# Letting planned transfers go by TensorE products instead of by queue order alone

## The chip, the cores and the metric

The kernel runs on one core of a Trainium2 chip. The metric is the device time of one execution in microseconds (us). A core has five engines with their own instruction streams: TensorE (PE, with its weight loads shown as PEld), VectorE (DVE), ScalarE (ACT), GpSimd (POOL) and SyncE (SP). Transfers are issued from the streams of SP, ACT and POOL, and move on 16 DMA engines.

## The reference

The kernel computes a DeltaNet attention block and then an MLP block. Cut to what matters:

```python
k_n = k / (norm(k) + 1e-06)                       # 4 batches, 8 heads, 768 steps, 48 wide
for t in range(S):
    y[t] = q[t] @ state
    v_old = k_n[t] @ state
    state = state + beta[t] * outer(k_n[t], v[t] - v_old)
x = y.transpose(0, 2, 1, 3).reshape(4, 768, 384)
xn = (x - mean(x)) / sqrt(var(x) + 1e-06) * g_ln
out = x + maximum(xn @ w_ch1, 0) @ w_ch2          # 384 -> 1536 -> 384
```

The two weight matrices arrive as 64-bit floats; the kernel makes 32-bit floats of them.

## The kernel before, in words

The 768 steps are cut into 12 chunks of 64 steps (`C = 64`). Inside a chunk the recurrence becomes matrix algebra: the products of the keys with each other (`gram`, line 963, stored to DRAM by the `gd<-gsb` transfers), the inverse of a unit triangular matrix per head, the chunk's corrected values (`recur`), the output `y` and the new state `s_all`. The chunks follow each other through `s_all`. Chunk 0 is inverted on PE (`first_inverse`, lines 915 and 930). For chunk 1 and for later pairs of chunks (`rows_inverse`) SP reads blocks of the stored products back (`gb<-gd`), ACT takes a root of their diagonal (`nrm_b`, line 1026), DVE goes through the rows one by one (lines 1045 and 1050, tiles `tmp` and `xb`), and the result goes out to DRAM (`xd<-xb`) and back in another layout (`xt<-xd`). Chunk 1 is joined from blocks of 16 (`blocks_join`, lines 1071 to 1089: `xnj` on DVE, then products on PE), the others from blocks of 32 (`join`, lines 1103 to 1125).

After `recur(c)` comes the MLP of the chunk's 256 tokens, `mlp(c)`: for chunks 0 to 2 the first product is plain (line 1483, ReLU on ACT in line 1492), later ones use a scheme of eleven products (line 1416); the second product is plain in chunk 0 (line 1505) and otherwise uses a scheme of seven products (line 1584), with sums on POOL and DVE (lines 1570, 1602, 1609).

The loads around the change are these. `load_raw` brings a chunk's keys to `kr` (for chunk 3 to `tb`), `load_padded` and `load_blocks` bring queries or keys to `tb`, `load_v` the values, `norms` reads the diagonal of the stored products (`ksum<-gd`), and eight small loads bring `beta_b`. SP issues nearly all of them. POOL issues the keys of the later chunks (`load_blocks(..., "Pool")`). ACT issues the twelve weight loads of 768 KB (`words<-in_moe_w_ch_dram` and two to `h_all`); `convert` turns each into weights with ACT, DVE and POOL (lines 730 to 748).

The order of all this is not written out by hand. Every piece of work is a `Step` of a `Line` with an engine, a cost and a priority. `schedule()` plays the engines and DMA queues through with costs in us and gives each step a planned start and end. A step may have `t0`, the time before which the plan doesn't start it:

```python
load_raw(c, pr=pr, t0=27.0)
...
load_padded(1, q, 1, ("SP", "SP"), pr=8.2, t0=42.0)
load_v(1, pr=8.1, t0=42.0)
...
t0 = {2: 85.0, 3: 105.0}.get(c, 0.7)
```

`emit()` (line 391) then issues the steps in the order of their planned starts, and `in_this_order` keeps that order on each engine. In the kernel before, `t0` has no other effect on the chip: an instruction whose operands and buffers are ready, and whose semaphore is free, runs as soon as its engine reaches it, whatever time the plan had for it. Each transfer from SP or ACT uses one of eight semaphores in turn, and a transfer waits until the one before it on the same semaphore has landed.

Of the kernel before, what the change touches and what calls it, by code (L numbers as in the profile page):

```python
# [23 lines left out]
@contextmanager  # L24
def in_this_order(tc):
    first = len(tc.nc.cur_bb.bb.instructions)
    last = {}
    yield last
    queued = None
    for ins in tc.nc.cur_bb.bb.instructions[first:]:  # L30
        if ins.engine not in ORDERED:
            continue
        if ins.engine in last:
            tc.add_manual_dep(
                ins, last[ins.engine].name,
                mybir.DependencyInfo(mybir.DependencyClass.NoSync, mybir.DependencyReason.DATA),
                reason="in_this_order",
            )
        last[ins.engine] = ins
        if "DMA" in type(ins).__name__ and ins.engine != mybir.EngineType.Pool:  # L40
            if queued is not None and queued.engine != ins.engine:
                tc.add_manual_dep(
                    ins, queued.name,
                    mybir.DependencyInfo(mybir.DependencyClass.NoSync, mybir.DependencyReason.DATA),
                    reason="in_this_order",
                )
            queued = ins
# [27 lines left out]
class Line:  # L75
# [313 lines left out]

        self.steps = every + self.fills  # L390

    def emit(self):
        for s in sorted(self.steps, key=lambda s: (s.start, s.n)):
            s.fn()


@with_exitstack
def kernel(
# [116 lines left out]
    line = Line()  # L515
# [1200 lines left out]
    for n, (p0, c, rows, cols) in enumerate(spots(BK, (0, 1))):  # L1716
        e, t0 = rows.start // C, c * C + cols.start
# [53 lines left out]
    if PLAN is not None:  # L1771
        PLAN.append(line)
    with in_this_order(tc):
        line.emit()


# [28 lines left out]
```

## Time and profile before

| | |
|---|---|
| runs | 558.52 us (median of 3; 556.83 to 559.81) |
| the profiled execution | 561.34 us |
| its span, first to last instruction | 559.0 us |
| PE busy / DVE / ACT / POOL | 525.5 / 370.3 / 192.1 / 253.2 us |
| granted TensorE clock, mean | 0.980 |
| PE share of the chain that ended last | 78% |
| DMA engines, mean rate | 98 GB/s |
| instructions | 23060 |

All times inside the execution are counted from its first instruction. In profile lines "SPq" stands for SP issuing a transfer; the time beside it is how long the issuing instruction took, not the transfer. Where a helper issues every transfer, all have its line, L555; the tile names tell them apart (`tb<-in_q_dram` is a load of queries to `tb`), without the buffers' numbers. A wait is named by what came last before the waiting instruction started.

### The profile page before, as it was taken

The page shows a single profiled execution, that of the slowest core. Times are in us where ns is not written, and L with a number is a line of the kernel's source. Part 1 is how long each engine was busy: PE and PEld are TensorE (multiplying, and loading weights), DVE is VectorE, ACT ScalarE, POOL GpSimd, SP SyncE. Part 2 cuts the span into 40 slices and gives each one's busy share as a digit, 9 for nine tenths or more (in the row PEclk, how much of TensorE's full clock was granted, in tenths as well). Part 3 has the DMA queues.
Part 4 walks back from the last instruction along what each step waited for, and adds up shares of the span by engine and source line. Part 5 has one row for each costly group of instructions (what it writes and reads, how often), then busy time and mean ns, then how long its engine had stood idle before and what let it go on. Part 6 is the DMA issues. An engine that isn't in the chain of part 4 may idle for free.

```text
span 559.0 us, 23060 instructions
## 1 busy us (share of the span) xinstructions
PE 525.5 (94%) x10060; PEld 478.8 (86%) x10060; DVE 370.3 (66%) x884; ACT 192.1 (34%) x452; POOL 253.2 (45%) x399
## 2 busy tenths in 40 slices
PE   7668869899998999899999999999999999999996
PEld 4547657678987899899999999999999999999996
DVE  5666549991689936889858968668777436253331
ACT  5667644232232324232323332513322224323030
POOL 5252337407885656267270352452352522426242
PEclk9898899999998999899999999999999999999999
DMA  9784784269454786553652543834404410111101
GB/s 177 265 158 128 195 219 64 44 149 168 55 86 71 139 195 86 106 100 83 162 77 50 99 81 77 191 46 81 94 15 103 106 30 33 32 48 40 28 1 28
DMA packets 195972, 54.65 MB, mean 98 GB/s; under 512 B 186136, under 2 KB 189344, under 8 KB 195872
## 3 DMA queue, kind: packets, MB, share of 16 engines
q1 hardware_dynamic: 190112, 40.39, 37.8%
q10 hardware_dynamic: 3552, 9.63, 5.0%
q0 software_dynamic: 2208, 3.17, 3.2%
q8 instruction: 78, 1.28, 1.0%
q14 instruction: 22, 0.18, 0.1%
HBM read 36.38 MB, written 16.78 MB: 95 GB/s over the span
## 4 chain that ended last, share of the span: by engine, by line
PE 78%; DVE 7%; DMA 6%; SPq 4%; issue 2%; ACT 1%; POOL 0%; DVEq 0%; POOLq 0%; ACTq 0%
PE f L1584 28%; PE f L1416 25%; PE f L1483 6%; SPq L555 4%; PE two L963 4%; DVE xb L1050 2%; DVE tmp L1045 2%; PE by L1222 2%; PE two L1215 2%; PE by L1160 2%; PE two L1160 2%; DMA gd<-gsb 2%; PE two L1232 2%; PE f L1505 1%; PE by L1115 1%
## 5 line engine op out<-in xcount | busy, mean ns | idle before, releaser
L1584 PE MATMUL f<-w_sb,h_all 128*128 128x192 f32 x396 | 95.0, 332 | 0.0
L1584 PE MATMUL f<-words,h_all 128*128 128x192 f32 x396 | 93.1, 328 | 0.0
L1570 POOL TENSOR_TENSOR h_all<-h_all 128x256 f32<-128x256 f32 x99 | 73.0, 742 | 43.3 <-PE f L1584 37.1
L1416 PE MATMUL f<-xnt,w_sb 128*128 128x128 f32 x648 | 88.8, 279 | 0.0
L1609 POOL TENSOR_TENSOR words<-h_all 128x128 f32<-128x128 f32 x66 | 30.3, 472 | 121.0 <-ACT h_all L1435 101.5
L1416 PEld LDWEIGHTS f<-xnt,w_sb 128*128 128x128 f32 x648 | 81.0, 193 | 0.7
L1438 DVE TENSOR_TENSOR h_all<-f,h_all 128x256 f32<-128x256 f32 x135 | 56.5, 421 | 34.1 <-PE f L1416 20.2
L1050 DVE TENSOR_TENSOR xb<-xb,tmp 128x60 f32<-128x60 f32 (+19 forms) x170 | 73.4, 432 | 5.8
L1045 DVE TENSOR_TENSOR tmp<-xb,gb 128x60 f32<-128x60 f32 (+19 forms) x170 | 65.3, 384 | 7.1 <-POOL xb L1034 4.5
L1584 PEld LDWEIGHTS f<-words,h_all 128*128 128x128 f32 x396 | 68.3, 190 | 0.4
L1584 PEld LDWEIGHTS f<-w_sb,h_all 128*128 128x128 f32 x396 | 66.4, 190 | 1.6 <-issue 0.2
L1483 PE MATMUL f<-xnt,w_sb 128*128 128x256 f32 x216 | 51.7, 390 | 0.0
L1483 PEld LDWEIGHTS f<-xnt,w_sb 128*128 128x128 f32 x216 | 41.3, 195 | 7.2
L555 POOL DMA_DIRECT2D tb<-in_k_dram x64 | 41.7, 656 | 7.0 <-DVE kt L943 5.8
L1602 DVE TENSOR_TENSOR o<-f,x 128x192 f32<-128x192 f32 x33 | 11.7, 355 | 47.7 <-PE f L1584 28.4
L1435 ACT ACTIVATE h_all<-f 128x256 f32<-128x256 f32 x54 | 20.6, 381 | 53.8 <-PE f L1416 28.0
L1584 PE MATMUL f<-w_sb,words 128*128 128x192 f32 x132 | 32.5, 330 | 0.6 <-DVE o L1602 0.6
L1602 POOL TENSOR_TENSOR o<-o,words 128x192 f32<-128x192 f32 x22 | 13.3, 624 | 38.6 <-DVE words L1602 38.6
L1492 ACT ACTIVATE h_all<-f 128x256 f32<-128x256 f32 x36 | 13.8, 383 | 38.2 <-PE f L1483 38.0
L1435 ACT ACTIVATE h_all<-h_all 128x256 f32<-128x256 f32 x54 | 22.2, 413 | 11.3 <-DVE h_all L1438 11.2
L748 POOL TENSOR_TENSOR w_sb<-words 128x768 uint32<-128x768 uint32 (+1 forms) x11 | 14.9, 1356 | 24.3 <-ACT words L738 19.4
L825 POOL TENSOR_TENSOR v<-v,knrm 128x768 f32<-128x768 f32 x11 | 16.7, 1518 | 16.7 <-DMA v<-in_v_dram 16.0
(235 smaller groups left out, 941.3 us busy)
## 6 DMA issues: line engine op xcount, KB each, us to landing
words<-in_moe_w_ch_dram ACTq DMA_DIRECT2D x10, 768.0 KB, 7.2
gd<-gsb SPq DMA_DIRECT2D x11, 512.0 KB, 3.9
v<-in_v_dram SPq DMA_DIRECT2D x24, 192.0 KB, 4.2
out_dram<-o SPq DMA_DIRECT2D x48, 96.0 KB, 2.3
kr<-in_k_dram SPq DMA_DIRECT2D x46, 96.0 KB, 3.0
xld<-xlt SPq DMA_DIRECT2D x9, 384.0 KB, 3.7
xnt<-xld SPq DMA_DIRECT2D x36, 96.0 KB, 3.0
gb<-gd SPq DMA_DIRECT2D x40, 64.0 KB, 3.7
```

Of the source, the lines that this page charges most:

```text
L555: add(eng, cost, lambda: QUEUE[eng].dma_start(out=out_, in_=in_), r, w, bulk=n * ns / 16e3, **kw)
L963: nc.tensor.matmul(pair[hp][half(e ^ (hp & n)), (g * NP + j) * C : (g * NP + j + 1) * C], kt[drows(hp), l], rt[drows(hp), i],)
L1045: nc.vector.tensor_tensor(out=t, in0=xv[:, 0:n, j : j + 1].to_broadcast([128, n, w]), in1=gv[:, j : j + 1, j + 1 : L].to_broadcast([128, n ...
L1050: nc.vector.tensor_tensor(out=rest, in0=rest, in1=t, op=ALU.subtract)
L1416: nc.tensor.matmul(wide(p[:, 128 * n : 128 * n + 128]), w[:, f : f + 128], r, start=start and n == 0, stop=stop, skip_group_check=True)
L1435: add("ACT", act(256), lambda: nc.scalar.activation(to[0], p, ACTF.Relu), pk, to[1])
L1438: add("DVE", dve(256), lambda: nc.vector.tensor_tensor(out=to[0], in0=ps(p), in1=y[0], op=op), [*pk, *y[1]], to[1])
L1483: nc.tensor.matmul(p[:, 0:TOK], w1_sb[:, t, f * 128 : (f + 1) * 128], xnt[:, t], start=(t == 0), stop=(t == KC - 1))
L1570: add(eng, cost, lambda: e.tensor_tensor(out=out_, in0=x, in1=y, op=op), r, w, port=2 if eng == "Pool" else 1, pr=-2)
L1584: lambda f=f, t=start and f == 0: nc.tensor.matmul(p[:, 0:D2], lhs(f), rhs[:, f], start=t, stop=(f == F2 - 1), skip_group_check=True),
L1602: lambda: e.tensor_tensor(out=out_, in0=a, in1=b_, op=ALU.add), r, w, pr=pr,
L1609: lambda f=f + i: e.tensor_tensor(out=s3[f], in0=one(0, 0)[0](f), in1=one(1, 0)[0](f), op=ALU.subtract),
```

## The change

`emit()` now adds waits. It walks through the steps in planned order and keeps the last instruction of each PE step with the step's planned end. For a transfer that has a set time (`t0` over 1 us), is not ACT's, and is planned to start less than 3 us after that time, it takes the latest of the last eight PE steps that end, in the plan, no later than the transfer starts, and makes the transfer wait for that step's last instruction on the chip. The plan itself, the order on each engine, and all computation stay as they are. 37 transfers get such a wait, 27 on SP and 10 on POOL. The wait is carried out by the issuing engine in its instruction stream.

```diff
-    def emit(self):
+    def emit(self, tc):
+
+        block = tc.nc.cur_bb.bb.instructions
+        gate, ends = None, []
         for s in sorted(self.steps, key=lambda s: (s.start, s.n)):
             s.fn()
+            if s.eng == "PE":
+                ends.append((s.end, block[-1]))
+            if s.bulk is not None and s.t0 > 1.0 and s.eng != "ACT" and s.start < s.t0 + 3.0:
+                gate = [i for e, i in ends[-8:] if e <= s.start]
+                if gate:
+                    tc.add_manual_dep(
+                        block[-1], gate[-1].name,
+                        mybir.DependencyInfo(mybir.DependencyClass.Sync, mybir.DependencyReason.DATA), reason="paced",
+                    )
...
-        line.emit()
+        line.emit(tc)
```

## The prediction

> **What bounds the kernel now.** I read the page's slices first, then the stretches between the places where they change, then who waits for whom in the part where TensorE is not full, and last the SP queue in order of time, because the change adds waits to it and to GpSimd's queue. The page's slices:
>
> ```profile
> span 559.0 us, 23060 instructions
> ...
> PE   7668869899998999899999999999999999999996
> ...
> DMA  9784784269454786553652543834404410111101
> ```
>
> TensorE (PE) is at six to eight tenths up to about 84 us and near full afterwards. In stretches (busy us of PE, PEld, DVE, ACT, POOL, then clock, DMA share, GB/s):
>
> ```profile
> 112.00:142.00 30.00, 30.00 (x406) 23.59 (x398) 17.14 (x41) 9.05 (x24) 12.98 (x23) 1.00 0.84 155
> 142.00:300.00 158.00, 153.78 (x3072) 142.47 (x3071) 124.39 (x279) 47.43 (x114) 91.52 (x141) 0.98 0.54 101
> ```
>
> From 112 us on PE has work all the time, so a microsecond won or lost before 112 us should reach the end one for one. Before it two stalls are the transfers' own (waits between 30 and 112 us: us in total, times, longest):
>
> ```profile
> DVE xnj L1071 <- DMA tb<-in_q_dram: 8.2, 1, 8.2
> ...
> PE f L1077 <- DVE xnj L1071: 4.4, 1, 4.4
> ACT nrm_b L1026 <- DMA gb<-gd: 4.3, 1, 4.3
> ...
> PE by L930 <- DVE nrm_b L1028: 3.7, 1, 3.7
> ```
>
> At 41.25 us ACT gets the last `gb` blocks, and PE stands for 3.7 us behind it. At 81.83 us DVE gets the `xt` blocks that `xnj` reads (the row names `tb`, which is queued right behind them), and PE stands for 4.4 us. The SP queue around both:
>
> ```profile
> 34.02 1.12 SPq L555 DMA_DIRECT2D gb<-gd  x2
> 35.23 1.84 SPq L555 DMA_DIRECT2D tb<-in_q_dram  x2
> 37.78 3.71 SPq L555 DMA_DIRECT2D v<-in_v_dram  x2
> 41.53 7.27 SPq L555 DMA_DIRECT2D beta_b<-in_beta_dram  x6
> ```
> ```profile
> 69.37 5.17 SPq L555 DMA_DIRECT2D xt<-xd  x8
> 74.64 1.16 SPq L555 DMA_DIRECT2D tb<-in_q_dram  x2
> 75.84 5.92 SPq L555 DMA_DIRECT2D v<-in_v_dram  x2
> ```
>
> Both late transfers are followed at once by loads that the plan sets for 42 and 46 us, and for 85 and 90 us: the chip issues them up to 7 and 10 us before their planned time, while its products run 4 to 10 us behind theirs.
>
> **What the change moves.** The order on every engine stays. 37 transfers (27 on SP, 10 on POOL) get a wait for a product. I matched each product with its matmuls in the trace and compared its end with the transfer's issue. 16 of the products are done before the issue: nothing moves. Four are 0.3 to 0.6 us late (one `kr` load at 28.5, one `v` half at 115.0, two k loads on POOL at 149.8 and 150.4). 17 bind, in three places:
> (a) two `tb`, two `v` and six `beta_b` loads, from 35.2-48.2 to 46.0-51.9 us (the products are L930's at 45.13+0.86, L915's at 47.2, L930's at 50.2 and 51.3, L771's at 51.9);
> (b) two `tb`, two `v` and two `ksum` loads, from 74.6-84.1 to 92.8-98.2 us, with four ungated `tb` loads among and behind them;
> (c) one `v` half, from 111.1 to 114.8 us.
>
> **Gain at gb.** In the DMA packets of the trace the last 64-byte packet of `gb` starts at 40.04, and the blocks land at 41.18: 1.14 us, while 192-byte packets of `tb` and `v` are moving. For the first six `gb` blocks the last packet is at 28.98 and the landing at 29.30: 0.32 us. I take the difference, 0.8 us. Bounds: nothing, if ACT's weight load at 33.91 is the cause alone; 3.7 us, PE's whole stall. **Gain at xt.** The last packet starts at 80.67, the landing is at 81.70: 1.03 against 0.32, so 0.7 us. ACT's weight packets in the same rings take 125 ns up to 80.2 and 145 to 260 ns from 80.25 to 81.4, when the 192-byte packets of `v` begin: a second sign that the followers cost something, and only at the end. Bounds: nothing to 4.4 us. I take the small values because the followers are the smaller part of the traffic: three weight loads of 768 KB (71.87, 72.37, 74.44) stay where they are, and `gb` has `kr` and `tb` loads ahead of it in its own queue.
>
> The Trainium skill ("DMA: Bandwidth & Descriptors", Queues, rings and completion order) says that an engine takes one ring's descriptors in order and turns between rings. That speaks against the change: a load issued later on SP's queue would not hold back an earlier one, and by it both gains are zero. The same page (Latency and other measured facts) gives HBM latency as 0.2 us on average and 2 us at high load; an estimate from that is up to 1.8 us for each landing, 3.6 us in all. No row here separates the two; the packets above lie between.
>
> **Cost of (a).** Behind the waiting loads on SP stand the store `gd` at 51.17, the store `gd` at 56.78 and the `gb` reads at 60.88. At 0.60 to 0.65 us for an issue, the four loads are out by 48.6, `beta_b` from 50.2 to 53.8, the first `gd` at 53.8 (2.6 us later), two more `beta_b` by 55.4. The second `gd` waits for ACT's copy that ends at 56.7 in any case, so SP has caught up with 1.3 us to spare. Readers: `tb` at 63.93 (L771), `v` at 74.04 (L825), `beta_b` at 82.46 (L1031), all over 10 us later. Cost 0, or 0.7 us if issues are held up as at 37.78, where one took 2.59 us. **Cost of (b).** SP has nothing else to do between 86.9 and 106.37 (`kr`). Ten issues from 92.8, the last two after `ksum` at 98.2, end near 100.7. Readers: `ksum` at 108.11 (L1144) and `tb` at 118.6 (L943); at 3.9 us to landing, 4.7 us are to spare. **Cost of (c).** The `gd` store behind it, released by ACT at 114.6, goes out about 0.9 us later, and `xd` at 124.27 waits for DVE's rows that end at 124.2. Cost 0. **POOL.** 0.3 us twice near 150 us, ahead of L1570, while PE has work: 0, at most 0.3. The 0.6 us at 28.5 shifts `kr`, `tb` and then `gb` issues, but their queue is backed up (one issue took 1.44 us at 31.18): 0, at most 0.6. **The waits themselves.** 20 more wait-only instructions (16 SP, 4 POOL) at 0.02 us in the rows of before: 0.3 us on SP, in its idle time.
>
> What takes up the delayed loads is free room, mean DMA share in the last column but one:
>
> ```profile
> 36.00:42.00 6.00, 2.37 (x70) 1.70 (x65) 2.29 (x6) 1.61 (x6) 0.31 (x2) 1.00 1.06 215
> 76.00:83.00 7.00, 2.63 (x57) 2.03 (x58) 1.17 (x3) 3.25 (x6) 0.24 (x1) 1.00 1.05 280
> 46.00:56.00 10.00, 8.85 (x336) 7.42 (x336) 7.32 (x29) 8.54 (x18) 2.59 (x3) 1.00 0.25 76
> 92.00:104.00 12.00, 10.90 (x337) 7.92 (x337) 11.41 (x25) 3.49 (x6) 9.57 (x15) 1.00 0.28 56
> ```
>
> **Sum.** -0.8 - 0.7 + 0 = -1.5 us. The profiled execution took 561.34 us (span 559.0 and 2.34 around it), so 559.8 on its own scale. The median of the runs is 558.52, 2.8 below it; I give the time on that scale: 557.0. What is late next: after 81.8 the rows of L1045 and L1050 on DVE (21.07 of 22 us busy from 90 to 112) move up with `xnj`, so the gain should not be lost there.
>
> **Rivals.** (1) The followers are the cause of both stalls. Then `gb` lands near its median of 3.0 us (issue at 34.69) and `xt` near its 2.5 us (issue at 72.68), and both PE stalls go: 3.7 + 4.4 = 8.0 us, to 550.5; with half of it 4.0 us, to 554.5. For it: DMA share over 1 in just these two windows, and 9.0 us to landing for the last `xt` block. Against it: the weight loads, which stay. It counts as faster from 2.8 us. Chance 0.37. (2) Slower: SP is not free in time in (a). The second `gd` takes 4.6 us to land (56.78 to 61.33) and its reader issues at 63.05, so from 1.7 us of lateness on every further microsecond goes through the `gb` reads, L1027, the `xd` store and `xt` to PE's stall at 78. Four of the ten issues held up as one `v` was (2.59 us in place of 0.62) put SP 7.9 us behind the 55.4 worked out above, so the second `gd` 6.5 us late, of which 4.8 reach the end: 563.3, or 561.8 if my gain is kept. Chance 0.18. (3) The waits change nothing, since the planned products end before the issue, as 16 of 37 do, or followers don't matter: 558.5. It shares 0.45 with my forecast.
>
> **How the numbers follow.** About 0.5% (2.8 us) is what a measurement of this kernel can tell from no change, so faster means under 555.7 and slower over 561.3. My forecast, with its own range 555.7 to 558.8, and rival 3 lie within: 0.45. Rival 1 gives 0.37 faster and rival 2 0.18 slower. For 8 in 10 the low end goes to 552.5 (rival 1 with 6 of its 8 us) and the high end to 560.8 (the bounds of the costs of (a), POOL and `kr`, 1.6 us together, with no gain, and part of rival 2).
>
> **What would show it.** Right: SP's `tb` and `v` at 46 and near 92 us with PE named as releaser; the wait of L1026 shorter by about 0.8 and that of L1071 by 0.7 us; the second `gd` still issued when ACT's copy ends; PE full after about 110 us. Wrong: either stall gone altogether or unchanged, `gd` or the `gb` reads issued later against ACT and DVE, L1144 or L943 waiting for a DMA, or new idle time of PE after 112 us.

## The result and the profile after

The changed kernel takes 558.96 us (median of 20 runs, 555.44 to 563.46); the kernel before, run beside it, takes 558.69 us (20 runs, 554.65 to 562.06). The ratio is 1.0009, with a 95% interval of 0.9984 to 1.0033: no difference that this measurement can tell. 557.0 us had been predicted, a ratio of 0.9973 to the median that it was worked out from. The call "no change" holds; the gain of 1.5 us behind it lies outside the interval. Runs more than 1.5% above the fastest of the same kernel count as slow and are left out of all medians and ratios below; none of these 40 is one.

The profiled execution of the changed kernel took 560.08 us, its span 557.7. Twelve lines were added ahead of the code in question, so L1071 of before is L1083 here, L1026 is L1038, L1077 is L1089, L930 is L942 and L963 is L975. First the page's slices of the kernel after:

```profile
span 557.7 us, 23080 instructions
...
PE   7669869999998999899999999999999999999996
...
DMA  9765863569455676453652544734414410111101
```

PE's row has the same shape: six to nine tenths in the first slices, then full. In the DMA row, with 14 us to a slice, the third digit (28 to 42 us) and the sixth (70 to 84) fell from 8 to 6, and the fourth, fifth and eighth (98 to 112) rose by 1, 1 and 3: the loads moved as ordered. The same stretches as before, from the kernel after (us, then PE, PEld, DVE, ACT, POOL busy, clock, DMA share, GB/s):

```profile
36.00:42.00 6.00, 2.40 (x70) 1.73 (x66) 2.32 (x6) 1.59 (x6) 0.44 (x1) 1.00 0.63 156
46.00:56.00 10.00, 8.89 (x344) 7.35 (x336) 8.98 (x29) 8.92 (x19) 3.04 (x3) 1.00 0.57 106
76.00:83.00 7.00, 2.28 (x45) 1.73 (x47) 1.25 (x3) 3.29 (x5) 0.24 (x1) 0.77 0.64 219
92.00:104.00 12.00, 10.50 (x336) 7.68 (x335) 11.41 (x25) 2.75 (x6) 9.15 (x14) 1.00 0.87 117
112.00:142.00 30.00, 29.53 (x361) 23.12 (x362) 16.71 (x40) 8.99 (x24) 12.99 (x23) 1.00 0.82 158
```

The reader is to set two columns against each other. The DMA share in the two stalls fell from 1.06 to 0.63 and from 1.05 to 0.64, and rose in the stretches that were to take the loads up. PE's busy time in the two stalls did not move: 2.40 of 6 us (2.37 before) and 2.28 of 7 us (2.63 before; the granted clock was 0.77 in this stretch, 1.00 before). The transfers went where the change sent them, and nobody waited less. The waits between 30 and 112 us, kernel after:

```profile
DVE xnj L1083 <- DMA xt<-xd: 9.7, 1, 9.7
...
ACT nrm_b L1038 <- DMA gb<-gd: 5.4, 2, 4.4
...
PE f L1089 <- DVE xnj L1083: 4.7, 1, 4.7
...
PE by L942 <- DVE nrm_b L1040: 3.6, 1, 3.6
```

The first row now names `xt` itself, since the `tb` loads that used to land with it are gone, but the wait is still there and ends at 81.75 us (81.83 before). ACT gets the last `gb` at 41.29 (41.25). PE's two stalls are 4.7 and 3.6 us (4.4 and 3.7). The SP queue, kernel after:

```profile
35.30 1.71 SPq L567 DMA_DIRECT2D gb<-gd  x2
46.15 1.32 SPq L567 DMA_DIRECT2D tb<-in_q_dram  x2
47.56 2.00 SPq L567 DMA_DIRECT2D v<-in_v_dram  x2
50.44 4.92 SPq L567 DMA_DIRECT2D beta_b<-in_beta_dram  x6
55.47 0.52 SPq L567 DMA_DIRECT2D gd<-gsb  x1
56.04 1.57 SPq L567 DMA_DIRECT2D beta_b<-in_beta_dram  x2
57.79 0.48 SPq L567 DMA_DIRECT2D gd<-gsb  x1
...
69.74 4.92 SPq L567 DMA_DIRECT2D xt<-xd  x8
93.03 0.88 SPq L567 DMA_DIRECT2D tb<-in_q_dram  x2
```

The two long gaps are SP's waits for PE products, as the waits of the SP queue between 40 and 104 us say:

```profile
SPq L567 <- PE f L1495: 18.1, 1, 18.1
SPq L567 <- PE f L1674: 9.6, 1, 9.6
```

For 9.1 us behind the `gb` reads and for 18 us behind the `xt` reads SP now issues nothing, and both still land as late as they did. So in these two profiles the loads behind them were not what made them late. What remained is what was in the queues ahead of them, above all the traffic of the other queue. DMA queues in the stretch from 73 to 80 us (packets, MB, share of 16 engines; q1 is SP's queue, q10 ACT's), kernel before and then kernel after:

```profile
q10 hardware_dynamic: 757, 2.22, 87.8%
q1 hardware_dynamic: 842, 0.06, 8.2%
```
```profile
q10 hardware_dynamic: 760, 2.24, 86.0%
q1 hardware_dynamic: 919, 0.06, 9.1%
```

ACT's weight loads take 86 to 88% of the engines' time in both, and SP's small packets get through at 1.1 to 1.2 for each weight packet of about 3 KB. In the 2 us before the weight packets begin, the trace of before shows 503 and 549 of the 64-byte packets of `xt` in a microsecond; beside them, from 75 to 79 us, 96 to 150.

### The profile page after: what moved, and what is told of

The parts are those of the page before. It is cut to its first block, busy times and chain, and to the rows that moved or that the text cites. A ratio compares the mean times of both kernels' runs of the same rounds, so it can differ in the third digit from the quotient of the medians.

```text
span 557.7 us, 23080 instructions
## 1 busy us (share of the span) xinstructions
PE 524.5 (94%) x10060; PEld 477.8 (86%) x10060; DVE 369.6 (66%) x884; ACT 191.7 (34%) x452; POOL 253.1 (45%) x399
## 4 chain that ended last, share of the span: by engine, by line
PE 80%; DVE 6%; DMA 5%; ACT 3%; issue 3%; SPq 2%; POOL 0%; ACTq 0%; DVEq 0%; POOLq 0%
PE f L1596 28%; PE f L1428 25%; PE f L1495 4%; PE two L975 4%; PE f L1517 3%; DVE xb L1062 2%; SPq L567 2%; PE by L1234 2%; PE by L1172 2%; PE two L1172 2%; PE two L1227 2%; DVE tmp L1057 2%; PE two L1244 2%; DMA xt<-xd 1%; PE by L1127 1%
## 5 line engine op out<-in xcount | busy, mean ns | idle before, releaser
L1450 DVE TENSOR_TENSOR h_all<-f,h_all 128x256 f32<-128x256 f32 x135 | 56.5, 421 | 34.1 <-PE f L1428 20.3
L1062 DVE TENSOR_TENSOR xb<-xb,tmp 128x60 f32<-128x60 f32 (+19 forms) x170 | 74.9, 441 | 5.8
```

Source lines behind the costliest of these rows:

```text
L1062: nc.vector.tensor_tensor(out=rest, in0=rest, in1=t, op=ALU.subtract)
L1450: add("DVE", dve(256), lambda: nc.vector.tensor_tensor(out=to[0], in0=ps(p), in1=y[0], op=op), [*pk, *y[1]], to[1])
```

## The experiments

My theory after the result: a small read on SP's queue that is issued behind one of ACT's 768 KB weight loads waits for that load, and what SP issues after the read does not matter. Rival: the loads that follow do matter, in one of the two places, and something in the change eats the gain. Second rival: the waits gain something and lose it again on SP. None of the kernels below leaves any computation out. Unless it says otherwise, ratios are to the kernel before on the same chip, with 95% intervals.

**The kernel before, in the changed code (one profile).** The code of the change with a condition that is never true, to see how far one profile differs from the next.

```diff
-            if s.bulk is not None and s.t0 > 1.0 and ...
+            if False and s.bulk is not None and s.t0 > 1.0 and ...
```

> The changed kernel with every new wait left out, so the program of the kernel before once more. It tells how much of the difference between the two profiles is chance: in the profile of the changed kernel the first gb read was issued 2.2 us later (25.63 against 23.46), ahead of any new wait. If that is chance, this run can have it at either place, and ACT's wait before L1038 and DVE's before L1083 end within 1 us of 41.25 and 81.83 all the same. If the followers on SP's queue held gb and xt back (rival 1), a run with the late first gb read should end ACT's wait about 2 us later than 41.3.

One run of 561.58 us, span 559.9. Last `gb` at 41.19, PE's stall behind it 3.6 us; `xnj` at 80.24, PE's stall 2.8 us. So the first stall repeats to 0.1 us, and the second varies by some 1.6 us from profile to profile: more than the 0.7 that I had predicted for it.

**Only the waits of place (a) (5 rounds).**

```diff
+            if s.t0 in (42.0, 46.0) and s.bulk is not None and s.t0 > 1.0 and ...
```

> Only the waits of the transfers planned for 42 and 46 us. My theory now: the followers cost gb nothing that can be seen and the waits push the second gd store about 1 us back, so the ratio to the kernel before is 1.000 to 1.003, with the second gd issued near 57.8 and the last xt block on its way when v and tb (still at 75 us) follow it, and DVE's wait ending at 81.5 to 82.5. Rival (followers hold gb back, and the gain was lost at SP): ACT's wait ends 0.8 us or more before 41.25 in this profile, ratio 0.998 or less.

Median 560.17 us, ratio 1.0026 (0.9989 to 1.0063). `gb` is used 6.35 us after its last issue with no follower behind it (6.56 before), PE's stall is 3.4 us, and the second `gd` goes out 1.6 us after ACT's copy that releases it. No gain in (a); a cost at the end isn't shown either, since the interval holds 1.

**Only the waits of place (b) (5 rounds).**

```diff
+            if s.t0 in (85.0, 90.0) and s.bulk is not None and s.t0 > 1.0 and ...
```

> Only the waits of the transfers planned for 85 and 90 us. With (a) left alone, SP's gd stores and gb reads are where they were, so the xt reads are issued from 69.4 as before and nothing but the followers is taken away from behind them. Rival (followers hold xt back): DVE's wait ends 0.7 us or more before 81.83, at 81.1 or earlier, and the ratio is 0.998 or less. My theory now (ACT's three weight loads hold xt back, the followers do not): DVE's wait ends at 81.4 to 82.2, PE's stall stays at 4.2 to 4.8 us, ratio 0.999 to 1.001.

Median 558.90 us, ratio 1.0003 (0.9962 to 1.0043): no gain in (b). Its profile, of a run of 556.52 us, is the surprise: PE's stall at `gb` is 0.5 us, though the followers of (a) are all there, ungated. Here are the rows of the SP queue, then of ACT's stream, then two of ACT's stream in the kernel before:

```profile
33.45 1.11 SPq L567 DMA_DIRECT2D gb<-gd  x2
34.66 1.32 SPq L567 DMA_DIRECT2D tb<-in_q_dram  x2
```
```profile
35.12 0.33 ACTq L567 DMA_DIRECT2D words<-in_moe_w_ch_dram  x1
...
36.98 1.14 ACT L885 COPY xt<-by 128x256 f32<-128x256 f32 x3
38.15 0.23 ACT L1038 ACTIVATE nrm_b<-gb 128x16 f32<-128x16 f32 x1
```
```profile
33.91 0.36 ACTq L555 DMA_DIRECT2D words<-in_moe_w_ch_dram  x1
...
41.25 0.23 ACT L1026 ACTIVATE nrm_b<-gb 128x16 f32<-128x16 f32 x1 [4.34 <-DMA gb<-gd]
```

In this run the last `gb` read went out at 34.12, a microsecond ahead of the weight load; in the kernel before it went out at 34.69, behind the weight load of 33.91. L1038 starts when ACT has finished its copies, with no wait for a DMA at all. A tenth of a microsecond behind `gb` the `tb` loads follow, and do no harm that shows: the last 64-byte packet of `gb` starts at 35.90, 1.8 us after the last issue (5.35 us in the kernel before).

**Three weight loads behind the `xt` reads (5 rounds).** The kernel before, without any wait; the weight loads of pieces 9 to 11 are issued by SP after the eight `xt` reads.

```diff
+        last = max(n for n, s in enumerate(order) if s.name == "xt1")
+        early = [s for s in order[:last] if s.name == "fetch9"]
+        order = [s for s in order[: last + 1] if s.name != "fetch9"] + early + order[last + 1 :]
...
-        add(eng, cost, lambda: QUEUE[eng].dma_start(...
+        add(eng, cost, lambda: QUEUE["SP" if kw.get("name", "") in ('fetch9', 'fetch10', 'fetch11') else eng].dma_start(...
```

> The kernel before, without any new wait, but the last three weight loads (pieces 9 to 11, 768 KB each, issued by ACT at 71.9, 72.4 and 74.4 us) are issued by SP, behind the eight xt reads; plan and order of all else as before. If ACT's weight loads hold xt back: the last xt block lands 2 to 3 us after its issue, at 75 to 76, PE's stall of 4.4 us before L1089 is gone, and the time falls by 3 to 4.4 us (ratio 0.992 to 0.995), less if DVE then waits for the later weights. If the followers on SP's queue hold it back (rival 1): they are still there, behind the weights, so the stall stays or shrinks by under 1 us, ratio 0.999 or more.

Median 556.71 us, ratio 0.9966 (0.9932 to 1.0), at the edge of what can be told from no change. The SP queue:

```profile
70.05 5.47 SPq L571 DMA_DIRECT2D xt<-xd  x8
75.61 1.43 SPq L571 DMA_DIRECT2D words<-in_moe_w_ch_dram  x3
77.56 0.94 SPq L571 DMA_DIRECT2D tb<-in_q_dram  x2
```

`xnj` starts 2.1 us after the last `xt` issue (9.2 us before), and PE's stall behind it is gone. The followers are not the old ones: three weight loads now come 0.1 us behind `xt` in its own queue, and the `tb` loads go out only at 77.56, after `xnj` has started at 77.14 (74.64 before, ahead of it). So this run shows that `xt` is early once ACT's loads are off it, and that 2.3 MB queued right behind it in its own queue do not hold it; it doesn't try `tb` and `v` beside it. Two smaller waits come up: ACT waits 3.4 us for the weights that now arrive later, and PE 1.7 us for ACT behind that. PE's stall at `gb`, which this edit leaves alone, is still 3.2 us.

**The weight load beside `gb` moved too (5 rounds), and the same with all 37 waits (5 rounds).** The first is the kernel of the last experiment with the weight load of piece 5, ACT's at 33.9 us, issued by SP right behind the last `gb` read. The second is the changed kernel with the same four loads moved.

```diff
-('fetch9', 'fetch10', 'fetch11')
+('fetch9', 'fetch10', 'fetch11', 'fetch5')
```

> The kernel before, with no waits, and four of ACT's twelve weight loads moved to SP's queue: the one that ACT issued at 33.9 us now goes right behind the last gb reads, and the three of pieces 9 to 11 go behind the eight xt reads. The followers (tb, v, beta_b; tb, v, ksum) stay where they are, as early as before. If a weight load in another ring is what holds gb and xt back (my theory after the runs so far): gb lands about 3 us after its last issue, so at 37 to 38.5 us, L1026's wait for it falls from 5.4 to 1-2.5 us, xt lands 2 to 3 us after its last issue, both PE stalls go or shrink to under 1.5 us, and the time falls by 3 to 7 us (ratio 0.988 to 0.995), less what ACT loses by waiting for weights that arrive later (it lost 1.7 us of PE with three loads moved). If the followers hold gb back (my first rival in the prediction): gb still lands near 41 us and only the gain with three loads moved is seen, ratio 0.997.

> The changed kernel (with all of its 37 waits) and the same four weight loads moved to SP's queue. If followers matter once the weight loads are out of the way, this is faster than the kernel with the loads moved alone by over 0.5% (3 us). If they do not matter: the same time as that kernel within 0.3%, with gb and xt landing as long after their last issue as there; if the wait at 46 us costs SP 1 us at the second gd store, it may be up to 1 us slower.

This pair is the test. Without waits: median 555.54 us, ratio 0.9955 (0.9923 to 0.9988). With waits: 555.32 us, ratio 0.9956 (0.9921 to 0.9992). The kernel before has 557.61 beside them. So the order of the weight loads is worth 2 us by the medians and 2.5 by the ratio, and the change under study, on top of it, nothing that shows: 0.2 us apart. Each of the two ratios is known to some 2 us only; the tighter bound on the change is its own interval above, which allows a gain of 0.9 us at the most. Both beat the kernel before; neither by as much as the 3 to 7 us that I had expected. The SP queue of the kernel without waits:

```profile
33.75 1.14 SPq L571 DMA_DIRECT2D gb<-gd  x2
35.00 0.38 SPq L571 DMA_DIRECT2D words<-in_moe_w_ch_dram  x1
35.48 2.42 SPq L571 DMA_DIRECT2D tb<-in_q_dram  x2
...
69.92 4.77 SPq L571 DMA_DIRECT2D xt<-xd  x8
74.79 1.43 SPq L571 DMA_DIRECT2D words<-in_moe_w_ch_dram  x3
```

A 768 KB load now stands 0.6 us behind the last `gb` issue (34.43), and `tb` 1.1 us behind it (0.5 before). Behind `xt` the `tb` loads go out at 76.75, after `xnj` has started at 76.33, as in the last experiment. ACT reads `gb` at 37.51 (L1042), as soon as its copies let it; the last packet of `gb` had started at 36.27, 1.8 us after the issue. With waits ACT does wait for `gb`:

```profile
36.14 1.11 SPq L571 DMA_DIRECT2D gb<-gd  x2
37.36 1.37 SPq L571 DMA_DIRECT2D words<-in_moe_w_ch_dram  x1
```
```profile
39.95 0.23 ACT L1042 ACTIVATE nrm_b<-gb 128x16 f32<-128x16 f32 x1 [1.59 <-DMA gb<-gd]
```

Here the last issue is at 36.81, and the use 3.1 us behind it. Where PE waits between 30 and 112 us in the kernel without waits:

```profile
PE f L979 <- issue: 3.4, 1, 3.4
PE f L1499 <- ACT h_all L1508: 3.1, 2, 2.8
...
PE f L1093 <- DVE xnj L1087: 0.3, 1, 0.3
PE by L946 <- issue: 0.2, 1, 0.2
```

Both old stalls are gone, 8.1 us together, and two others stand in their place, 6.5 us together (0.7 us of the first in the kernel before). The second is ACT's wait for the later weights, one row of ACT's stream:

```profile
79.97 0.88 ACT L746 ACTIVATE words<-words 128x768 f32<-128x768 f32 x1 [4.03 <-DMA words<-in_moe_w_ch_dram]
```

The first had been hidden under the stall at `gb`; more of it below.

**One more profile of each kernel.** They try the rule that the table below gives.

> The kernel before once more, for one more profile. The profiles so far suggest: where ACT's weight load of about 34 us is issued before the last gb reads, gb lands 6.8 to 7.4 us after that weight load's issue (41.2 to 42.3 us); where it is issued after them, gb lands 3 to 4 us after its own last issue (38.2 us in one profile) and the span is 4 to 5 us shorter. The same is expected here: one of the two, and the span by which one. If the followers were the cause, the order of these two issues would not matter.

> The changed kernel once more, for one more profile, with the same rule: gb lands 6.8 to 7.4 us after ACT's weight load of about 34 us if that was issued before the last gb reads, 3 to 4 us after its own last issue if not; the waits keep the followers away in either case and should not matter. The second gd store is again about 1 us later than ACT's copy releases it.

Before: 558.13 us, span 556.4. This time the `gb` reads (34.14) went ahead of the weight load (36.29), L1038 started at 39.31 as soon as ACT's copies let it, and PE's stall at `gb` is 0.5 us. The span is 2.6 us shorter than in the first profile, not 4 to 5: `xt` was still caught by its weight loads. After: 560.62 us, span 557.9; the weight load (35.7) ahead of `gb` (39.28), L1038 at 43.49, 7.8 us after the weight load and so 0.4 us outside what I had expected, and the second `gd` 1.5 us after ACT's copy ended. All ten profiles, in us from the first instruction:

| kernel | followers of `gb` held | weight load issued | last `gb` issued | its last packet starts | `gb` used (ACT) | last `xt` issued | `xnj` starts | first `s_all` | span |
|---|---|---|---|---|---|---|---|---|---|
| before | no | 33.9 | 34.7 | 40.0 | 41.25 | 72.7 | 81.8 | 110.5 | 559.0 |
| before, again | no | 33.9 | 34.7 | 40.0 | 41.19 | 72.5 | 80.2 | 109.6 | 559.9 |
| before, third | no | 36.3 | 34.1 | 35.8 | 39.31 (ACT busy) | 74.2 | 80.1 | 107.8 | 556.4 |
| only (b) | no | 35.1 | 34.1 | 35.9 | 38.15 (ACT busy) | 71.8 | 77.4 | 104.9 | 554.8 |
| after | yes | 34.0 | 36.6 | 40.7 | 41.29 | 74.2 | 81.8 | 109.3 | 557.7 |
| after, again | yes | 35.7 | 39.3 | 42.9 | 43.49 | 76.6 | 84.0 | 111.5 | 557.9 |
| only (a) | yes | 35.1 | 35.9 | 41.6 | 42.29 | 75.9 | 82.3 | 110.1 | 560.6 |
| three loads moved | no | 34.8 | 35.1 | 40.5 | 41.62 | 75.1 | 77.1 | 106.5 | 555.5 |
| four loads moved | no | SP, behind `gb` | 34.4 | 36.3 | 37.51 (ACT busy) | 74.3 | 76.3 | 105.8 | 552.9 |
| four moved, waits | yes | SP, behind `gb` | 36.8 | 39.3 | 39.95 | 74.1 | 77.6 | 106.7 | 553.4 |

Where the weight load was issued first, `gb` is used 6.9 to 7.8 us after that load's issue (6.9 to 7.3 with followers, 7.1 to 7.8 without), and its last packet starts 0.3 to 1.5 us behind the weight load's last. Where `gb` was first, its last packet starts 1.7 to 2.5 us after its own last issue. In neither group does holding the followers back bring `gb` earlier. With `xt` the weight loads don't set the end so strictly: its last packet comes from 3.7 us ahead of to 0.3 us behind the last one of the three loads, but 4.9 to 8.0 us after its last issue where ACT's loads run beside it, and 1.5 to 2.9 us where they have been moved.

## Why the prediction was right or wrong

**What bounds the kernel.** Right. PE is full after 112 us, and what is won ahead of it reaches the end to some 2 us either way: from the first `s_all` to the end of the span the ten profiles have 446.4 to 450.6 us, while the first `s_all` itself lies anywhere from 104.9 to 111.5.

**What moves.** Right, to 0.8 us or better: `tb` at 46.15 (46.0 predicted), `beta_b` from 50.44 (50.2), `tb` at 93.03 (92.8), the first `ksum` of (b) at 98.98 (98.2), the `v` half of (c) at 114.08 (114.8).

**Gain at gb, 0.8 us.** Wrong: nothing that shows. The reading of the 1.14 us from last packet to landing was not the fault. From the start of the last 64-byte packet to ACT's use of `gb` it takes 1.15 to 1.22 us in the three profiles that have the weight load first and the followers behind, and 0.60 to 0.69 us in the three with the followers held, so about half a microsecond there goes with the followers. The step that failed is to count it as a gain, with the last packet taken as fixed. That packet came later instead: in the trace after it starts at 40.69 (40.04 before), 1.5 us behind the weight load's last packet (39.18), where it had been 0.5 us behind it (39.50). In this run the read had also been issued later (36.57 against 34.69). The fairest pair is "only (a)" and "before", where the last read goes out 0.8 us behind the weight load in both: counted from the weight load's issue, the last packet starts after 6.45 us with waits and 6.13 without, and `gb` is used after 7.1 and 7.3 us. Why the last packet comes later without followers stays open. I had priced the end of a transfer whose length was set by the weight load; my own argument against the followers, the weight load at 33.91 and its lower bound of nothing, was the right value to take.

**Gain at xt, 0.7 us.** Wrong: nothing (`xnj` 0.08 us earlier, PE's stall 0.3 us longer). The same step: from the last packet to the start of `xnj` it is 0.84 us after the change and 1.16 before (0.71 to 0.84 and 0.76 to 1.16 over all profiles with ACT's loads in place, two ranges that overlap), but the last packet starts 0.24 us later (80.91 against 80.67). The "second sign" failed with it. Without the followers the weight load of that moment does end 0.84 us sooner (last packet at 80.66 instead of 81.50), but half of that is its earlier issue (74.02 against 74.44), and in the kernel before `xt` had its last packet ahead of that end in any case.

So the call "no change" was in part luck: it came out because both gains in the sum were small, and neither was there.

**The rule that spoke against the change.** By the Trainium skill ("DMA: Bandwidth & Descriptors", Queues, rings and completion order), an engine takes one ring's descriptors in order and turns between rings. The runs agree, as far as they can tell: 0.2 us between the two kernels with the weight loads moved, and `gb` done 1.8 us after its last issue with `tb` 0.1 us behind it in the queue. The rule's other half, the turns between rings, fits what holds the small reads back: in the trace, where SP's and ACT's packets stand as two queues, about one small packet gets through per weight packet (842 beside 757, 919 beside 760). No run here shows in what portions the engines turn. I had put the followers' cost between this rule's zero and an estimate from loaded latency; for the time of the kernel the zero was the answer.

**Cost of (a), 0 us.** Right at the end, wrong on the way. SP was to be free 1.3 us before the second `gd`; it issued that store at 57.79, 1.5 us after ACT's copy had ended at 56.26. The mis-sized term is the price of an issue: the six `beta_b` took 0.82 us each instead of 0.60 to 0.65, the two `v` 1.0 each, and the first `gd` went out at 55.47 instead of 53.8. The lateness is inside the 1.7 us from which rival 2 was to count, and the `xt` reads began 0.37 us later than before (69.74 against 69.37). In the pair with the weight loads moved, the first `xt` also goes out 0.37 us later with waits and the medians differ by 0.2 us, the kernel with waits being the faster: no cost that can be measured.

**Cost of (b), (c), POOL, the waits.** No cost shows: the rows of the waits hold no reader of `ksum` or `tb` that waits for these loads, and PE is busy 29.53 of the 30 us from 112 on (30.00 before). The missing 0.47 us are one stop of PE at L1172, which the profile puts down to no transfer.

**The rivals.** Rival 1 (the followers are the whole cause) had too high a chance: the DMA share over 1 that spoke for it was followers filling the room that the late reads left: without them it fell to 0.63 and 0.64, and the reads were as late. Its price was also too high. With both stalls really gone, the time fell by 2 to 2.5 us and not by 8: the first profile lay 2.8 us over its median, and other stalls came up. Rival 2's mechanism was there (SP late by 1.5 us) but stayed under its threshold. Rival 3, the waits change nothing, is what happened.

## What to carry to other kernels

The two late transfers here were held up by large loads of another queue and not by what came behind them in their own. So where a small transfer lands late, list first the other queues' large loads that are in flight with it, and try moving those behind it. A DMA share near 1 during a stall did not say who caused it here: the loads queued later filled the engines. A cost that is read at the end of a transfer (last packet to landing) is a gain only if the last packet stays where it is. Before a stall is priced from one profile, look at how that run stands to the median, and at what the stall hides.

## What the runs showed that I had not expected

The order of two issues on different queues changes from run to run: the last `gb` reads go ahead of or behind ACT's weight load, and `gb` is used 1.9 to 3.1 us sooner if ahead (38.15 and 39.31 against 41.19 and 41.25, same transfers). The two spans with `gb` ahead are also the shorter ones (556.4 and 554.8 against 559.0 and 559.9); four profiles are too few to say how much of the kernel's spread comes from it. A change of 2 to 2.5 us is smaller than what one profile can differ from the next (spans of 554.8 to 560.6 here, for programs whose times can't be told apart).

Where `gb` comes early, PE meets another stop. Rows of PE in the kernel with four loads moved and no waits:

```profile
43.02 0.99 PE L979 MATMUL f<-kt 48*64 48x64 f32 x52
47.38 0.59 PE L979 MATMUL f<-kt 48*64 48x64 f32 x11 [3.37 <-issue]
```

After 52 of 64 products PE stands for 3.4 us and waits for no data. With waits it stands 2.95 us at the same product, in the profile with only (b) 2.5, in the kernel before 0.74, where PE gets there 4 us later. Each of these traces has one 16 KB packet of the instruction queue near it: in the kernel with four loads moved it starts at 44.69 us and takes 1.33, inside PE's stop; in the kernel before it starts at 46.10, 1.95 us ahead of PE's arrival. In all seven profiles with the stop, PE goes on 2.6 to 2.9 us after that packet starts, although it gets there anywhere from 44.0 to 48.3 us; in the three without the stop, PE is at this product 2.7 to 3.6 us after the packet starts. That PE waits for this packet is what the rows suggest; no run took it away. It would explain why most of the 3.7 us at `gb` could not be cashed in.
